# The second MLP's first product of tokens 1024 to 3071 in seven block products for eight, weight block sums through DRAM

## The chip, the cores and the metric

The kernel runs on one core of a Trainium2 chip. The metric is the device time of one execution in microseconds (us). A core has a matrix engine (TensorE, PE in the profile), three engines for elementwise work (VectorE or DVE, ScalarE or ACT, GpSimd or POOL), a queue engine that only starts transfers (SyncE, SP), an on-chip memory (SBUF, 128 partitions) and eight accumulation banks for PE (PSUM). Each engine executes its own instructions in a fixed order and waits on semaphores for the others.

## What is computed

The reference, cut to its core:

```python
def _moe_ref(x, w_gate, w_val, w_out):        # d_ff 1536
    gate = 1.0 / (1.0 + np.exp(-(x @ w_gate)))
    val = x @ w_val
    return (gate * val @ w_out).astype(np.float32)

def _moe2_ref(x, w_in, w_out):                # d_ff 2048
    h = x @ w_in
    g = h * (1.0 / (1.0 + np.exp(-1.702 * h)))
    return (g @ w_out).astype(np.float32)

def reference(**kwargs):
    ...
    attn_out = _attn_ref(**attn_kwargs)
    B, H, S, D = attn_out.shape
    x = np.ascontiguousarray(attn_out.transpose(0, 2, 1, 3)).reshape(B * S, H * D)
    x = _moe_ref(x=x, **moe_kwargs)
    return _moe2_ref(x=x, **moe2_kwargs)
```

`_attn_ref` is attention in chunks of 32 queries over a short context (4 batches, 8 heads, 768 positions of 64 values). It gives x with 3072 tokens of 512 values. The first MLP multiplies sigmoid(x w_gate) by x w_val and projects back to 512; the second computes h = x w_in with 2048 columns, h * sigmoid(1.702 h), and projects back to 512.

## The kernel before

**Precision.** PE multiplies rounded operands, so each float32 operand is cut into a high part and a low part, and each product is three matmuls: high by high, high by low, low by high. The inputs arrive as 64-bit numbers; `convert` loads 512 KB of a weight (`raw`) and turns it on ACT, DVE and POOL into a slot `w` that holds the highs and the lows of 128 rows or columns (lines 258 to 291: L258 load, L262 and L272 ACT, L267, L276 and L281 DVE, L286 the high on ACT, L291 the low on DVE or POOL).

**Tiling.** Tokens are handled in six blocks of 512. A matmul has 128x128 weights and 512 columns of tokens. For each slice f of 128 hidden columns, `first_product` makes 12 matmuls: 8 for the highs of the weight (L742), 4 for the lows (L749), over four parts of the depth of 512. In the second MLP there are 16 slices in each block. `gated` then takes the product from its bank: sigmoid on ACT (L766, `sig`), multiplication by the product on DVE (L769, into `sig`), the high `gh` on ACT (L772), the low `gl` (L776) on POOL in the second MLP's block 0, on DVE elsewhere. `gemm4` is the second product of a slice, 12 matmuls (L720), added up over the 16 slices in four banks. `sig`, `gh` and `gl` have two buffers each, and the first products of the second MLP alternate between two banks.

**Between the MLPs.** The first MLP's result goes from its banks by ACT (L937) to DRAM (`y_dram`, L941) and comes back a block at a time in `y_in`: four loads (L957), four highs on ACT (L960, `xh`), four lows on POOL (L963, `xl`). After the last block ACT (L1045) and DVE (L1043) empty the banks and SP stores the output (L1049).

**Order.** Every step is handed to the class `Schedule` as a task with an engine, a modelled duration and the data that it reads and writes. A planner then gives each engine a fixed order: among the ready tasks of an engine it takes the one with the earliest due time. A PE product's due time is the sum of the modelled durations of the products handed in before it (`clock[0]`), and other tasks inherit theirs from what needs them. The planner's durations decide the order alone; on the chip each engine goes through its order and waits where something isn't there. The weights of the second MLP are converted while the first MLP's products run; its slots come free as the first MLP's weights are used up.

The functions that the change touches and what calls them, with the profile's line numbers:

Of the kernel before, what the change touches and what calls it, by code (L numbers as in the profile page):

```python
# [1103 lines left out]
```

## Time and profile before

| what | value |
|---|---|
| device time, median of 3 runs | 1220.63 us (1219.94 to 1221.95) |
| span of the profiled execution, first to last instruction | 1217.7 us |
| PE, busy share of the span | 98% |
| DVE, busy share | 51% |
| ACT, busy share | 39% |
| POOL, busy share | 10% |
| mean granted clock of PE | 0.994 |

The page gives the profiled execution's span, and its device time is not listed apart from it; the median of the runs lies 2.9 us above the span. The busy shares are means over stages that differ: attention lies mostly in the first half, the conversion of the second MLP's weights ends at about 693 us, and the second MLP runs from there to the end. "Granted clock" is the clock that the chip gave PE, with 1.00 for 2.4 GHz. A duration in the timeline is that of one instruction, and instructions of one engine that follow each other overlap a little, so that their spacing is shorter than their duration.

### The profile page before, as it was taken

How to read it: one execution, taken by the hardware profiler on the slowest of the kernel's cores; microseconds unless marked ns; L12 is line 12 of the kernel's file. 1: busy time of each engine (PE TensorE's matmuls, PEld its weight loads, DVE VectorE, ACT ScalarE, POOL GpSimd, SP SyncE). 2: the span in 40 equal slices, each digit the busy share in tenths (PEclk: the TensorE clock that was granted, in tenths of full speed). 3: DMA queues.
4: the chain of work that ended last, by engine and by line, in shares of the span. 5: the costliest groups of instructions: out<-in, count | busy, mean ns of one | idle time of the engine just before them, and what ended most of it. 6: DMA issues, size and time to landing. Idle time of an engine off the chain costs nothing.

```text
span 1217.7 us, 18791 instructions
## 1 busy us (share of the span) xinstructions
PE 1195.5 (98%) x7448; PEld 997.8 (82%) x7448; DVE 622.6 (51%) x1282; ACT 481.0 (39%) x779; POOL 123.6 (10%) x112
## 2 busy tenths in 40 slices
PE   5899999999999999999999999999999999999998
PEld 4688899988888888888888888888888888888886
DVE  7898858883778448617888611222222222322322
ACT  5698734442334224413667632222222222322222
POOL 1221200000000000000211232110000100100000
PEclk9799999999999999999999999999999999999999
DMA  9566333333133113300555310100100100200001
GB/s 229 131 201 181 100 81 54 53 54 70 34 52 79 24 22 58 80 1 23 152 185 169 121 52 1 53 18 1 65 5 1 69 1 1 70 1 1 35 1 36
DMA packets 169673, 78.01 MB, mean 64 GB/s; under 512 B 136176, under 2 KB 156912, under 8 KB 169584
## 3 DMA queue, kind: packets, MB, share of 16 engines
q1 hardware_dynamic: 166128, 70.51, 22.6%
q10 hardware_dynamic: 3456, 6.29, 1.4%
q8 instruction: 58, 0.95, 0.3%
q14 instruction: 31, 0.25, 0.1%
HBM read 64.18 MB, written 12.58 MB: 63 GB/s over the span
## 4 chain that ended last, share of the span: by engine, by line
PE 96%; DVE 2%; DMA 1%; ACT 1%; issue 0%; SPq 0%; DVEq 0%
PE bank L742 35%; PE bank L720 21%; PE bank L749 18%; PE bank L917 16%; PE bank L656 2%; PE bank L506 2%; PE bank L596 1%; DMA raw<-in_moe_w_gate_dram 0%; DVE pw L574 0%; PE bank L397 0%; DMA qn<-in_q_dram 0%; PE bank L389 0%; DVE e L526 0%; DVE mx L523 0%; DVE sm L563 0%
## 5 line engine op out<-in xcount | busy, mean ns | idle before, releaser
L742 PE MATMUL bank<-xh,w 128*128 128x512 f32 (+1 forms) x1040 | 383.5, 374 | 2.8 <-ACT w L286 1.6
L742 PE MATMUL bank<-xl,w 128*128 128x512 f32 (+1 forms) x1040 | 382.3, 373 | 0.0
L769 DVE TENSOR_TENSOR sig<-bank,sig 128x512 f32<-128x512 f32 (+1 forms) x178 | 117.4, 660 | 410.4 <-ACT sig L766 328.9
L749 PE MATMUL bank<-xh,w 128*128 128x512 f32 (+1 forms) x1040 | 260.1, 374 | 0.0
L766 ACT ACTIVATE sig<-bank 128x512 f32<-128x512 f32 (+1 forms) x178 | 102.4, 575 | 386.7 <-PE bank L749 378.1
L720 PE MATMUL bank<-w,gh 128*128 128x512 f32 x768 | 236.5, 389 | 0.0
L742 PEld LDWEIGHTS bank<-xh,w 128*128 128x128 f32 x1040 | 195.7, 188 | 39.1 <-ACT w L286 2.3
L742 PEld LDWEIGHTS bank<-xl,w 128*128 128x128 f32 x1040 | 195.9, 188 | 34.3
L749 PEld LDWEIGHTS bank<-xh,w 128*128 128x128 f32 x1040 | 186.0, 188 | 35.0
L772 ACT ACTIVATE gh<-sig 128x512 fp32r<-128x512 f32 (+1 forms) x178 | 108.1, 607 | 187.0 <-DVE sig L769 170.2
L720 PEld LDWEIGHTS bank<-w,gh 128*128 128x128 f32 x768 | 144.1, 188 | 29.9
L917 PE MATMUL bank<-gh,w 128*128 128x512 f32 (+1 forms) x656 | 158.2, 365 | 0.0
L776 DVE TENSOR_TENSOR gl<-sig,gh 128x512 fp32r<-128x512 f32 (+1 forms) x162 | 110.2, 680 | 84.7 <-ACT gh L772 73.0
L720 PE MATMUL bank<-w,gl 128*128 128x512 f32 x384 | 149.4, 389 | 0.0
L917 PEld LDWEIGHTS bank<-gh,w 128*128 128x128 f32 x656 | 114.4, 189 | 19.8
L720 PEld LDWEIGHTS bank<-w,gl 128*128 128x128 f32 x384 | 72.1, 188 | 15.0
L631 DVE STREAM_TRANSPOSE pt<-raw 32x256 f32<-32x256 f32 x184 | 80.1, 435 | 2.8
L917 PE MATMUL bank<-gl,w 128*128 128x512 f32 (+1 forms) x328 | 80.4, 367 | 0.0
L917 PEld LDWEIGHTS bank<-gl,w 128*128 128x128 f32 x328 | 56.8, 189 | 9.9
L574 POOL TENSOR_TENSOR raw<-e,sm 96x448 f32<-96x448 f32 x23 | 23.2, 1007 | 405.6 <-DVE sm L566 405.6
L963 POOL TENSOR_TENSOR xl<-f,xh 128x512 fp32r<-128x512 f32 x24 | 31.0, 1301 | 276.6 <-ACT xh L960 276.6
L286 ACT ACTIVATE w<-f 128x512 fp32r<-128x512 f32 x68 | 42.7, 640 | 13.2 <-DVE f L281 9.1
(84 smaller groups left out, 822.1 us busy)
## 6 DMA issues: line engine op xcount, KB each, us to landing
raw<-in_moe_w_out_dram SPq DMA_DIRECT2D x24, 512.0 KB
raw<-in_moe_w_in_dram SPq DMA_DIRECT2D x16, 512.0 KB
y_dram<-f ACTq DMA_DIRECT2D x24, 256.0 KB
f<-y_dram SPq DMA_DIRECT2D x24, 256.0 KB
out_dram<-f SPq DMA_DIRECT2D x23, 256.0 KB
vn<-in_v_dram SPq DMA_DIRECT2D x24, 240.0 KB
f<-in_q_dram SPq DMA_DIRECT2D x276, 16.0 KB
raw<-in_moe_w_gate_dram SPq DMA_DIRECT2D x8, 512.0 KB
```

Of the source, the lines that this page charges most:

```text
L286: nc.scalar.activation(slots[slot][:, 0, :], ft, AF.Copy)
L506: nc.tensor.matmul(bk[c * CH : (c + 1) * CH, p * KW : (p + 1) * KW], T["qt"][r, p, c * CH : (c + 1) * CH], T["kt"][r, p, c, :], start=True ...
L631: nc.vector.transpose(T["pt"][r * CH : (r + 1) * CH, :, c * CH : (c + 1) * CH], T["pn"][c * CH : (c + 1) * CH, :, kb * CH : (kb + 1) * CH],)
L720: nc.tensor.matmul(ps_out, a, c, start=(first and i == 0 and j == 0), stop=(last and i == n - 1 and j == 2),)
L742: nc.tensor.matmul(bank[bk][:, :n], w[:, 0, ts[t]], x[xb][:, t, c0 : c0 + n], start=t == 0 and x is xhs, stop=False)
L749: nc.tensor.matmul(bank[bk][:, :n], w[:, 1, ts[t]], xhs[xb][:, t, c0 : c0 + n], start=False, stop=t == NK - 1)
L766: nc.scalar.activation(sig[:, :n], bank[src_sig][:, :n], AF.Sigmoid, scale=scale)
L769: nc.vector.tensor_tensor(out=sig[:, :n], in0=bank[src_val][:, :n], in1=sig[:, :n], op=ALU.mult)
L772: nc.scalar.activation(gh[:, :n], sig[:, :n], AF.Copy)
L776: eng.tensor_tensor(out=gl[:, :n], in0=sig[:, :n], in1=gh[:, :n].bitcast(F32), op=ALU.subtract)
L917: nc.tensor.matmul(bank[Y[m]][:, c0 : c0 + n], w[:, wi, m * P : (m + 1) * P], g[:, :n], start=f == 0 and j == 0 and c0 == 0, stop=f == F1 ...
L963: nc.gpsimd.tensor_tensor(out=xls[xb][:, m, :], in0=st[:, :BLK], in1=xhs[xb][:, m, :].bitcast(F32), op=ALU.subtract)
```

## The change

The first product of blocks 0 and 1 of the second MLP stays as it is. Blocks 2 to 5 are taken as two superblocks of two blocks. For two slices (a pair j, eight of them) and two blocks, the depth of 512 in two halves, the product is one of 2x2 blocks of weights with 2x2 blocks of tokens. Winograd's form of Strassen's scheme needs seven products (`m1` to `m7`, `part_product`, 6 matmuls each) of sums of the blocks for the eight of the direct way.

- `combine(j)` makes the sums of weight blocks of a pair, once: POOL adds highs and lows back to whole numbers (`cw_a`, `cw_b`), DVE makes four sums of 256 columns (`cw_s`) and, after ACT has cut the highs (`cw_h`), the lows (`cw_l`). SP writes three ready blocks and the four sums of each pair to DRAM (`wc_dram`).
- `fetch` brings the seven blocks of a pair back, 256 KB each, into a ring of 14 that lies in freed slots, once for each superblock.
- `x_prep` makes the sums of token blocks for a superblock: 8 loads, 8 subtractions on DVE, 14 highs on ACT, 14 lows on POOL and DVE.
- In the loop over pairs the products share banks, so that PE does part of the additions by accumulating. `snap` copies a bank to SBUF on ACT, `plus` adds another bank on DVE; `gate2` makes the sigmoid and the multiplication. The first block's two results go on to `halves` (`gh` and `gl`, as before), the second block's are kept as `gBs` until the pairs are through; then their halves and second products follow.

```diff
-    def gemm4(b, f, i):
+    def gemm4(f, i, banks, row, end=False, after=()):
...
+    NBP = 2
+    NSB = (NB2 - NBP) // 2
+    NPR = F2 // 2
+    NMP = 7
...
+    STEPS = {"m1": (MA11, XB11), "m5": (MS1, XT1), "m6": (MS2, XT2), "m2": (MA12, XB21),
+             "m3": (MS4, XB22), "m7": (MS3, XT3), "m4": (MA22, XT4)}
+    SEQ = ["m1", "m5", "m6", "m2", "m3", "m7", "m4"]
...
+    def combine(j):
+        s0, s1 = slot_in2[2 * j], slot_in2[2 * j + 1]
+
+        def whole(x, s):
+            def fn():
+                w = slots[s]
+                nc.gpsimd.tensor_tensor(out=cw[x], in0=w[:, 0, :].bitcast(F32), in1=w[:, 1, :].bitcast(F32), op=ALU.add)
+
+            add("pool", c_pool(512), fn, r=[("w", s, 0), ("w", s, 1)], w=["c" + x])
...
+        def sums():
+            wa, wb, s = cw["wa"], cw["wb"], cw["s"]
+            tt = nc.vector.tensor_tensor
+            tt(out=s[:, 0, :], in0=wb[:, :H2], in1=wb[:, H2:], op=ALU.add)
+            tt(out=s[:, 2, :], in0=wa[:, :H2], in1=wb[:, :H2], op=ALU.subtract)
+            tt(out=s[:, 1, :], in0=s[:, 0, :], in1=wa[:, :H2], op=ALU.subtract)
+            tt(out=s[:, 3, :], in0=wa[:, H2:], in1=s[:, 1, :], op=ALU.subtract)
+
+        def high():
+            nc.scalar.activation(cw["h"], cw["s"], AF.Copy)
...
+        for m, s, c in ((MA11, s0, 0), (MA12, s0, H2), (MA22, s1, H2)):
+            put(m, 1, None, lambda s=s, c=c: slots[s][:, :, c : c + H2].bitcast(F32), [("w", s, 0), ("w", s, 1)])
+        put(MS1, 4, 0, lambda: cw["h"].bitcast(F32), ["cwh"])
+        put(MS1, 4, 1, lambda: cw["l"].bitcast(F32), ["cwl"])
+
+    for j in range(NPR):
+        combine(j)
...
+    def part_product(g, m, bk, first):
+        h = (g * NMP + SEQ.index(m)) % NRH
+        x = STEPS[m][1]
+
+        def fn():
+            w = ringh[h]
+            for k in range(2):
+                for wl, xl in ((0, 0), (0, 1), (1, 0)):
+                    o = wl * H2 + k * P
+                    nc.tensor.matmul(
...
-    for b in range(NB2):
+    for b in range(NBP):
...
+            part_product(g, "m1", a, True)
+            snap("s1", a)
+            part_product(g, "m5", e, True)
+            snap("s5", e)
+            if fill:
+                gemm4(*fill.pop(0))
+            part_product(g, "m6", a, False)
+            snap("s2", a)
+            part_product(g, "m2", bb, True)
+            plus("s1", bb)
+            ia = gate2(lambda: work["s1"], "s1")
+            part_product(g, "m3", e, False)
+            plus("s2", e)
+            gate2(lambda: work["s2"], "s2", 2 * j)
+            part_product(g, "m7", a, False)
+            plus("s5", a)
+            gate2(lambda: work["s5"], "s5", 2 * j + 1)
+            if fill:
+                gemm4(*fill.pop(0))
+            part_product(g, "m4", a, False)
+            ic = gate2(lambda a=a: bank[a], ("bank", a))
+            if g + 2 < NSB * NPR:
+                fetch(g + 2)
...
+        for f in range(F2):
+            gemm4(*fill.pop(0))
+            i = halves(lambda f=f: gbs[f], ("gB", f))
+            fill.append((f, i, ob, row + BLK, end))
```

In the changed file `combine`'s whole sums are L1093, its quarter sums L1103 to L1106, its highs L1109 and lows L1113, its writes L1126 and L1128; `fetch` is L1234, `part_product` L1248, `snap` L1260, `plus` L1264, the multiplication of `gate2` L1292, the low of `halves` L1278.

**POOL in block 0 of the second MLP.** The slices' `gl` take two buffers in turn (`gl_86`, `gl_87`); the last row is that of slice 8. Before, from block 1's second-last `xl` on:

```order
L963 TENSOR_TENSOR xl_735<-f_79,xh_734 128x512
L776 TENSOR_TENSOR gl_86<-sig_82,gh_84 128x512
L963 TENSOR_TENSOR xl_735<-f_80,xh_734 128x512
L776 TENSOR_TENSOR gl_87<-sig_83,gh_85 128x512
L776 TENSOR_TENSOR gl_86<-sig_82,gh_84 128x512
L776 TENSOR_TENSOR gl_87<-sig_83,gh_85 128x512
L776 TENSOR_TENSOR gl_86<-sig_82,gh_84 128x512
```

The same stretch in the changed kernel, from slice 5's `gl` on:

```order
L776 TENSOR_TENSOR gl_87<-sig_83,gh_85 128x512
L1093 TENSOR_TENSOR cw_b<-w_642 128x512
L963 TENSOR_TENSOR xl_736<-f_80,xh_735 128x512
L1093 TENSOR_TENSOR cw_a<-w_644 128x512
L1093 TENSOR_TENSOR cw_b<-w_646 128x512
L776 TENSOR_TENSOR gl_86<-sig_82,gh_84 128x512
L1093 TENSOR_TENSOR cw_a<-w_648 128x512
L1093 TENSOR_TENSOR cw_b<-w_650 128x512
L776 TENSOR_TENSOR gl_87<-sig_83,gh_85 128x512
L1093 TENSOR_TENSOR cw_a<-w_652 128x512
L1093 TENSOR_TENSOR cw_b<-w_654 128x512
L776 TENSOR_TENSOR gl_86<-sig_82,gh_84 128x512
```

The last row is the `gl` of slice 8. Since the last conversion (L291) 28 instructions stand ahead of it: 16 whole sums, 8 `gl` and 4 `xl`; before, 12 stood ahead of it.

**DVE from the last conversions on.** Before, the multiplications of the second MLP's slices 0, 1, 2 follow the last conversions directly:

```order
L776 TENSOR_TENSOR gl_87<-sig_83,gh_85 128x512
L291 TENSOR_TENSOR w_653<-f_77,w_653 128x512
L281 SCALAR_TENSOR_TENSOR f_78<-f_78,raw_75 128x512
L769 TENSOR_TENSOR sig_82<-bank_66,sig_82 128x512
L291 TENSOR_TENSOR w_654<-f_78,w_654 128x512
L769 TENSOR_TENSOR sig_83<-bank_67,sig_83 128x512
L769 TENSOR_TENSOR sig_82<-bank_66,sig_82 128x512
```

In the changed kernel the sums and lows of the weights stand between them:

```order
L291 TENSOR_TENSOR w_655<-f_78,w_655 128x512
L1103 TENSOR_TENSOR cw_s<-cw_b 128x256
L1104 TENSOR_TENSOR cw_s<-cw_a,cw_b 128x256
L1105 TENSOR_TENSOR cw_s<-cw_s,cw_a 128x256
L1106 TENSOR_TENSOR cw_s<-cw_a,cw_s 128x256
L769 TENSOR_TENSOR sig_83<-bank_67,sig_83 128x512
L1113 TENSOR_TENSOR cw_l<-cw_s,cw_h 128x512 x2
L1103 TENSOR_TENSOR cw_s<-cw_b 128x256
L1104 TENSOR_TENSOR cw_s<-cw_a,cw_b 128x256
L1105 TENSOR_TENSOR cw_s<-cw_s,cw_a 128x256
L1106 TENSOR_TENSOR cw_s<-cw_a,cw_s 128x256
L769 TENSOR_TENSOR sig_82<-bank_66,sig_82 128x512
```

The multiplication of slice 1 now stands behind pair 0's sums, and that of slice 2 (last row) behind pair 1's.

**PE in the loop over pairs (changed kernel only).** `bank_67` is the bank of `m1`, `m6`, `m7`, `m4` here, `bank_73` that of `m5` and `m3`, `bank_66` that of `m2`. The rows run from the end of a second product (slice 8's, weight `w_641`) over `m6`, `m2`, `m3` and `m7` to the next:

```order
L720 MATMUL bank_71<-w_641,gl_86 128x512
L1248 MATMUL bank_67<-sb_x_6708,sb_r_7658 128x512 x3
L1248 MATMUL bank_67<-sb_x_6762,sb_r_7658 128x512 x3
L1248 MATMUL bank_66<-sb_x_6657,sb_r_7697 128x512 x3
L1248 MATMUL bank_66<-sb_x_6681,sb_r_7697 128x512 x3
L1248 MATMUL bank_73<-sb_x_7322,sb_r_7697 128x512 x3
L1248 MATMUL bank_73<-sb_x_7346,sb_r_7697 128x512 x3
L1248 MATMUL bank_67<-sb_x_7387,sb_r_7728 128x512 x3
L1248 MATMUL bank_67<-sb_x_7433,sb_r_7728 128x512 x3
L720 MATMUL bank_68<-w_643,gh_85 128x512 x2
```

After that second product `m4` writes into `bank_67`, which `plus` of `s5` reads once `m7` is through. Before, a slice there had 12 matmuls of L742 and L749 and then 12 of L720.

## Rows read from the trace of the kernel before

**Rows 1.** The page: span, busy time by engine, slices of PE and its clock.

```profile
span 1217.7 us, 18791 instructions
PE 1195.5 (98%) x7448; PEld 997.8 (82%) x7448; DVE 622.6 (51%) x1282; ACT 481.0 (39%) x779; POOL 123.6 (10%) x112
...
PE   5899999999999999999999999999999999999998
...
PEclk9799999999999999999999999999999999999999
```

**Rows 2.** The page: chain that ended last, shares by engine and line.

```profile
PE 96%; DVE 2%; DMA 1%; ACT 1%; issue 0%; SPq 0%; DVEq 0%
PE bank L742 35%; PE bank L720 21%; PE bank L749 18%; PE bank L917 16%; PE bank L656 2%; PE bank L506 2%; PE bank L596 1%; DMA raw<-in_moe_w_gate_dram 0%; DVE pw L574 0%; PE bank L397 0%; DMA qn<-in_q_dram 0%; PE bank L389 0%; DVE e L526 0%; DVE mx L523 0%; DVE sm L563 0%
```

**Rows 3.** Stretches: length, busy time (count) by engine, clock, DMA share, GB/s.

```profile
28.00:44.00 16.00, 11.28 (x96) 9.70 (x96) 14.39 (x33) 7.29 (x14) 3.15 (x3) 0.57 0.14 54
...
630.00:730.00 100.00, 100.00 (x443) 82.81 (x442) 54.67 (x88) 58.02 (x89) 23.62 (x18) 1.00 0.37 116
730.00:830.00 100.00, 100.00 (x443) 82.81 (x442) 20.54 (x29) 24.91 (x42) 16.75 (x13) 1.00 0.06 22
830.00:930.00 100.00, 100.00 (x443) 82.81 (x442) 28.25 (x40) 26.57 (x44) 5.13 (x4) 1.00 0.06 22
```

**Rows 4.** Timeline of PE at 701: start, duration, engine, line, operands, count.

```profile
701.82 0.62 PE L720 MATMUL bank<-w,gh 128*128 128x512 f32 x2
```

**Rows 5.** Chain that ended last, its longest pieces: start, duration, what.

```profile
785.40 2.72 PE bank L720 x12
...
1207.90 5.47 PE bank L720 x24
```

**Rows 6.** Timeline of POOL, from 599 to 707 us.

```profile
599.82 1.30 POOL L963 TENSOR_TENSOR xl<-f,xh 128x512 fp32r<-128x512 f32 x1 [2.01 <-ACT xh L960]
...
677.70 1.29 POOL L291 TENSOR_TENSOR w<-f,w 128x512 fp32r<-128x512 f32 x1 [6.83 <-ACT w L286]
686.85 1.30 POOL L291 TENSOR_TENSOR w<-f,w 128x512 fp32r<-128x512 f32 x1 [7.86 <-ACT w L286]
...
705.28 1.29 POOL L776 TENSOR_TENSOR gl<-sig,gh 128x512 fp32r<-128x512 f32 x1 [5.56 <-ACT gh L772]
706.53 1.29 POOL L963 TENSOR_TENSOR xl<-f,xh 128x512 fp32r<-128x512 f32 x1
```

**Rows 7.** Timeline of DVE, from 599 to 702 us.

```profile
599.86 1.81 DVE L291 TENSOR_TENSOR w<-f,w 128x512 fp32r<-128x512 f32 x1
...
628.73 0.43 DVE L267 TENSOR_SCALAR raw<-raw 128x512 int32<-128x512 int32 x1 [1.76 <-DMA raw<-in_moe_w_in_dram]
...
678.45 0.69 DVE L769 TENSOR_TENSOR sig<-bank,sig 128x512 f32<-128x512 f32 x1 [1.79 <-PE bank L749]
...
688.95 0.68 DVE L776 TENSOR_TENSOR gl<-sig,gh 128x512 fp32r<-128x512 f32 x1
689.55 0.68 DVE L291 TENSOR_TENSOR w<-f,w 128x512 fp32r<-128x512 f32 x1
...
701.81 0.69 DVE L769 TENSOR_TENSOR sig<-bank,sig 128x512 f32<-128x512 f32 x1 [4.75 <-ACT sig L766]
```

**Rows 8.** Groups by line and shape: count, busy us, mean ns, idle before.

```profile
L526 DVE TENSOR_TENSOR e<-bank,mx 96x256 f32<-96x256 f32 x64 | 23.8, 410 | 0.1
...
L772 ACT ACTIVATE gh<-sig 128x512 fp32r<-128x512 f32 x158 | 99.8, 632 | 166.0 <-DVE sig L769 160.7 <-PE bank L720 3.9 <-ACT f L937 1.4
L766 ACT ACTIVATE sig<-bank 128x512 f32<-128x512 f32 x158 | 94.7, 599 | 365.0 <-PE bank L749 364.7
L410 ACT ACTIVATE kt<-bank 128x384 f32<-128x384 f32 x9 | 4.5, 501 | 5.3 <-PE bank L397 5.2
L411 ACT ACTIVATE kt<-bank 128x96 f32<-128x96 f32 x9 | 2.2, 249 | 0.0
```

**Rows 9.** Timeline of SP's queue: a weight load is issued.

```profile
624.88 0.38 SPq L258 DMA_DIRECT2D raw<-in_moe_w_in_dram  x1
```

More of the change, by code (lines that the diff above doesn't have):

```diff
@@ L1028, in gemm4 @@
             fn,
-            [("w", s, 0), ("w", s, 1), ("gh", i), ("gl", i)] + after,
-            [("bank", O[b][tt]) for tt in range(TT)],
+            [("w", s, 0), ("w", s, 1), ("gh", i), ("gl", i), *after],
+            [("bank", k) for k in banks],
         )
@@ new lines, in fetch, with fn @@
+    def fetch(g):
+        for p, m in enumerate(SEQ):
+            h = (g * NMP + p) % NRH
+            src = g % NPR * NMP + STEPS[m][0]
+            def fn(h=h, src=src):
+                nc.sync.dma_start(out=ringh[h].bitcast(F32), in_=wc_dram[src])
+            kr = [("wc", g % NPR, STEPS[m][0], x) for x in range(2)]
+            add("sp", 0.45, fn, r=kr, w=[("ring", h)], nbytes=P * 512 * 4)
+    def part_product(g, m, bk, first):
+        h = (g * NMP + SEQ.index(m)) % NRH
+        x = STEPS[m][1]
+        def fn():
+            w = ringh[h]
+            for k in range(2):
+                for wl, xl in ((0, 0), (0, 1), (1, 0)):
+                    o = wl * H2 + k * P
+                    nc.tensor.matmul(
+                        bank[bk],
+                        w[:, o : o + P],
+                        xt[x, k][:, xl, :],
+                        start=first and k == 0 and wl == 0 and xl == 0,
+                        stop=k == 1 and wl == 1,
+                        skip_group_check=not first,
+                    )
+        product(c_mm(512, 6), fn, [("ring", h)] + xkey(x), [("bank", bk)])
@@ L1067 @@
                 gemm4(*pend)
-            if f == 0 and b + 1 < NB2:
+            if f == 0 and b + 1 < NBP:
                 y_in(b + 1, (xb + 1) % 2)
-            pend = (b, f, i)
-    gemm4(*pend)
+            pend = (f, i, O[b], b * BLK)
+    nsig[0] = ngh[0] = ng[0]
+    x0 = NB % 2
+    add("none", 0.0, open_x0, w=xkeys(x0) + xkey(XB11) + xkey(XT1))
+    add("none", 0.0, open_work, w=KCW + KYS + ["s1", "s2", "s5", ("gB", 0), ("gB", 1)])
+    homes = [(m, k) for m in (XB21, XT2, XB22, XT3, XT4) for k in range(2)]
@@ new lines @@
+    assert 2 * len(left[NRH // 2 :]) + 2 == 8
+    add("none", 0.0, open_x1b, w=xkeys(1 - x0) + [("gB", f) for f in range(8, 16)])
+    sets = [[6, 7, 0, 1], [2, 3, 4, 5]]
+    assert sorted(O[NBP - 1]) == sets[1]
+    fill = [pend]
+    fetch(0)
+    fetch(1)
+    for sb in range(NSB):
+        a0, e, bb, a1 = sets[sb % 2]
+        oa = sets[1 - sb % 2]
+        ob = [bb, e, a0, a1]
+        row = (NBP + 2 * sb) * BLK
+        ready = []
+        for j in range(NPR):
+            g = sb * NPR + j
+            a = (a0, a1)[j % 2]
+            part_product(g, "m1", a, True)
[21 more added lines that the diff above has]
+                fetch(g + 2)
+            fill += [(2 * j, ia, oa, row), (2 * j + 1, ic, oa, row)]
+        if sb + 1 < NSB:
+            x_prep(NBP + 2 * sb + 2)
+        end = sb == NSB - 1
+        for f in range(F2):
+            gemm4(*fill.pop(0))
+            i = halves(lambda f=f: gbs[f], ("gB", f))
+            fill.append((f, i, ob, row + BLK, end))
```

152 lines of the change are left out of this document (147 added, 5 removed).

## The prediction

> **What bounds the kernel now.** I read the page first: TensorE (PE) is busy for 98% of the span, no other engine for more than 51%, and the granted clock stands at its upper level in all slices but one [rows 1]. The chain that ended last is 96% PE, and its largest line, L742, is the first products [rows 2]. Then I read the busy time by stretches: in the second MLP each stretch of 100 us holds 100.00 us of PE, with VectorE (DVE), ScalarE (ACT) and GpSimd (POOL) at 5 to 58%; in the stretch 630 to 730, with five times the DMA traffic of the next (116 against 22 GB/s), PE runs just as full [rows 3]. So from about 630 us the time is matmuls times their spacing, and whatever is taken out there shortens the span, unless PE then begins to wait. The clock's mean fell to 0.57 (1.00 is the level of 2.4 GHz, 0.50 that of 1.2) only at 28 to 44 us, where PE was busy for 11.28 of 16 us [rows 3]; waits of a microsecond or two are not of that kind, and I charge no clock.
>
> The spacing: the first second-product of the second MLP starts at 701.82 [rows 4], the last group starts at 1207.90 and lasts 5.47, to 1213.37 [rows 5]. The second MLP has 6 blocks x 16 slices x 24 = 2304 matmuls, of which 48 run before 701.82 (the first products of four slices). (1213.37 - 701.82) / 2256 = 0.2267 us each, and 12 then take 2.72, as the chain shows [rows 5].
>
> **The change, part by part.** *Removed:* for each pair of slices of two blocks, 8 half-depth products of 6 matmuls become 7: 48 to 42. With 8 pairs and 2 superblocks this is 16 x 6 = 96 matmuls, 96 x 0.2267 = **21.8 us**. Nothing else on PE changes in number: the new ones are 128x128 by 512 columns too, with one weight load each, as before.
>
> *Added on POOL, DVE and ACT in block 0 of the second MLP:* `combine` builds four sums of weight blocks for each of 8 pairs. This is 16 whole sums on POOL, 32 quarter sums (256 columns) and 16 lows (512) on DVE, 8 highs of 1024 columns on ACT. All stand in the queues where block 0's gating stands, and block 0 cuts its `gl` on POOL. In the order the POOL op that cuts `gl` of slice 8 now has 28 others ahead of it that may start only after the last weight conversion (16 sums, 8 earlier `gl`, 4 `xl`); before it had 12 of them. The price hangs on one thing: whether DVE and POOL can work at once. The rows say no, for DVE instructions that read two operands from SBUF: POOL's L963 starts at 599.82 and lasts 1.30 [rows 6], and DVE's L291, begun at 599.86, takes 1.81 [rows 7], where the same line alone takes 0.68 (689.55) [rows 7]; the surplus of 1.13 is about what was left of the POOL instruction. A DVE multiplication that reads one operand from PSUM took its normal 0.69 at 678.45 [rows 7], inside POOL's L291 at 677.70 [rows 6]. The sums and lows are of the held kind. So I add POOL and DVE up, as one queue.
>
> This queue starts when POOL's last conversion ends, 686.85 + 1.30 = 688.15 [rows 6], and ends with `gl` of slice 8. It holds 29 POOL instructions, the quarter sums of seven pairs (28) and the lows of six (12), since the whole sums of pair 7 wait for the quarter sums of pair 6, and these for the lows of pair 5. By durations: 29 x 1.29 [rows 6] + 28 x 0.41 (L526, 256 columns [rows 8]) + 12 x 0.68 [rows 7] = 37.4 + 11.5 + 8.2 = 57.1, so 745.2. By spacings of instructions back to back, which overlap a little: POOL 1.25 (705.28 to 706.53 [rows 6]); DVE 0.60 (688.95 to 689.55 [rows 7]), thus 0.08 less than a duration, and 0.33 for 256 columns: 36.3 + 9.2 + 7.2 = 52.7, so 740.9. PE needs that `gl` in the second product of slice 8: in the new order the fifth slice's first product stands where the first second-product stood, so at 701.82 if nothing waits, and 170 matmuls later the matmul reads `gl`: 701.82 + 170 x 0.2267 = 740.4. The stall is thus between **0.5** and **4.8 us**. To that comes ACT's high of 1024 columns, which stands between sums and lows: from 96 columns in 0.249 and 384 in 0.501 [rows 8], 0.875 ns a column, some 1.06 us. Where POOL has its next whole sums and gating to do meanwhile it is covered, else not; I take it as covered in six of the first seven pairs, which leaves 1.1; uncovered in all seven it is 7.4. I take durations, not spacings, since at each change between the two engines there is a handover and no overlap: 4.8 + 1.1 = **5.9 us**, bounds 0.5 and 4.8 + 7.4 = 12.2. What is late after that is only PE; the `gl` of slices 9 to 15 follow with one POOL instruction per 24 matmuls (5.4 us).
>
> The Trainium skill (Advanced Engine Details and Errata, VectorE Performance Modes) says that GpSimd and VectorE share a second SBUF port and hold each other up, but only for VectorE instructions in a two-port mode, and its table gives tensor_tensor none. By that rule the sums would run beside POOL. The row of L291, a TENSOR_TENSOR, at 1.81 speaks against the narrow reading; the section GPSIMD Details of the same page has the wider one (two SBUF inputs), which agrees. By the narrow rule the time would be that of the first rival below.
>
> A smaller wait lies ahead of it: the multiplication of slice 2 stands behind the quarter sums of pair 1 on DVE. It ran at 701.81 before [rows 7] and the fifth slice's first product reuses its bank; 0 to 1 us, inside the same stall and not added to it.
>
> *Added DMA:* 8 x (3 x 256 + 2 x 512) KB written, 14.7 MB, and 16 x 7 x 256 KB read, 29.4 MB. In the loop 7 x 256 KB come per pair of 66 matmuls (42 first, 24 second), 15.0 us: 123 GB/s, like the 116 GB/s beside which PE ran full [rows 3]. The ring holds two pairs, so a fetch has about one pair, 15 us, where a 512 KB load took from its issue at 624.88 [rows 9] to its use at 628.73 [rows 7], 3.9 us. Cost nothing, covered by the other half of the ring. The writes of ready weights stand among the raw loads in SP's queue, each behind a conversion that those loads wait for anyway: 0 to 1 us on conversions that are used much later. Nothing.
>
> *Added in the loop:* per pair DVE has 9 instructions of 0.69 (6.2 us) and ACT 9 of about 0.6 (5.4 us), in 15.0 us of PE. The tightest place is `m4`, which writes into the bank that `plus s5` still reads. `m2`, `m3`, `m7` take 1.36 us each. From the end of `m2`: `plus s1` to 0.69, sigmoid (0.60 [rows 8]) to 1.3, `plus s2` from 1.36 to 2.05, the multiplication to 2.74, `plus s5` to 3.43. PE has the second product of 12 (2.72) after `m7`, and comes to `m4` at 2.72 + 2.72 = 5.44. Slack 2.0 us: hidden. `m6` waits for the snapshot of `m1` and has `m5` and a second product between, 4.1 us against 0.6: hidden. `x_prep` (8 loads, 8 subtractions, 14 highs, 14 lows) runs in block 1, where DVE had 28.25 us of work in 100 (830 to 930 [rows 3]), for its first call, and under sixteen second products (43.5 us) for the second: hidden. The final run of second products needs one high (0.63 [rows 8]) and one low (0.68 [rows 7]) per 2.72 us: hidden. Without this cover each place would cost its own microsecond or two per pair.
>
> **Sum.** The profiled execution has a span of 1217.7; the median is 1220.63, so 2.9 us lie around the span, and I keep them. 1220.6 - 21.8 + 5.9 = **1204.7** (a span of 1201.8).
>
> **The rivals.** *A, the sums are hidden:* POOL and DVE do not hold each other, or the alternation overlaps more than I say, and 0.5 to 0.9 us stay: 1220.6 - 21.8 + 0.5 to 0.9 = 1199.3 to 1199.7. For it: the lower bound by spacings. Against: the 1.81. *B, the stall is larger:* ACT's highs lie bare in each pair, and with semaphores between three engines it exceeds 12.2: 1211 to 1218. For it: the chain sums, high, lows, sums has three engines and single buffers. Against: POOL has other work to do meanwhile. *C, slower:* in each of the 16 pairs `m4` waits for `plus s5`, because DVE takes its work in a fixed order and the multiplication ahead waits for ACT, which itself stands behind a snapshot or a high of the pair before. With the slack of 2.0 used up and exceeded by 1.5 us: 16 x 1.5 = 24 us, so 1204.7 + 24 = 1228.7; it turns the change to no gain from (21.8 - 5.9) / 16 = 1.0 us per pair. Against: the engines in that loop are idle for half of the time. *D, it doesn't take 96 away:* excluded, the new order has 6328 PE matmuls against 6424.
>
> **Chances.** Forecast case 0.60 (1200 to 1211), A 0.22, B 0.11, C 0.07, of which 0.03 end within 0.2% of before. This kernel's measurement can tell 0.2%, 2.4 us, from no change. Faster 0.93, same 0.03, slower 0.04. The range takes in A and the forecast case with its upper bound, 1220.6 - 21.8 + 12.2 = 1211.0, and a little of B: 1198.5 to 1212.5.
>
> **What would show it.** PE idle for 3 to 10 us in all between 700 and 750, ended by POOL's `gl` (L776) or a DVE multiplication (L769), and none to speak of after 760; L1093 on POOL and L1103 to L1113 on DVE with means above 1.29, 0.41 and 0.68; L1248 672 times, L742 1568 and L749 784 times; the clock 1.00 throughout. I am wrong if PE waits in the loop of pairs (for `sb_r`, a late fetch, or for L1264 in front of `m4`), or if L1093 and L1113 have their plain durations while PE still waits.

## The result and the profile after

The changed kernel takes 1208.45 us (median of 4 runs, 1207.04 to 1209.51) against 1221.29 of the kernel before: 12.8 us less, a ratio of 0.9897 with a 95% interval of 0.9883 to 0.9911. The forecast was 1204.7 with a range of 1198.5 to 1212.5. The profiled execution has a span of 1207.7.

The page of the changed kernel: span, busy time, shares of the chain that ended last (to compare with [rows 1, 2]).

```profile
span 1207.7 us, 19184 instructions
PE 1180.2 (98%) x7352; PEld 982.2 (81%) x7352; DVE 712.2 (59%) x1406; ACT 522.2 (43%) x847; POOL 153.3 (13%) x128
...
PE 90%; DVE 5%; ACT 2%; issue 1%; DMA 1%; POOL 0%; DVEq 0%; SPq 0%; ACTq 0%; POOLq 0%
```

PE has 96 instructions fewer (7352 for 7448), and is still busy for 98%. What is new is the second engine in the chain: DVE with 5% where it had 2%, and ACT with 2% where it had 1%. So PE now waits for them somewhere. The busy time by stretches says where (columns as in [rows 3]: length, busy time of PE, PE's weight loads, DVE, ACT and POOL, clock, DMA share, GB/s):

```profile
700.00:720.00 20.00, 19.22 (x85) 15.58 (x84) 16.13 (x22) 9.21 (x15) 13.98 (x10) 1.00 0.74 250
720.00:740.00 20.00, 19.57 (x87) 15.84 (x86) 13.88 (x18) 7.98 (x13) 16.38 (x13) 1.00 0.44 145
740.00:747.00 7.00, 5.07 (x23) 3.82 (x21) 6.39 (x8) 2.18 (x3) 5.45 (x4) 1.00 0.45 151
747.00:752.00 5.00, 4.70 (x14) 3.75 (x15) 3.52 (x7) 1.58 (x2) 1.80 (x2) 0.66 0.56 189
752.00:760.00 8.00, 8.00 (x37) 6.60 (x36) 0.69 (x1) 1.48 (x3) 1.12 (x2) 1.00 0.66 210
...
940.00:950.00 10.00, 10.00 (x46) 8.29 (x45) 3.18 (x5) 2.94 (x5) 0.00 (x0) 1.00 0.37 109
...
980.00:990.00 10.00, 9.24 (x41) 7.32 (x41) 7.93 (x9) 5.59 (x11) 6.42 (x4) 1.00 0.50 135
990.00:1000.00 10.00, 9.04 (x39) 6.82 (x38) 9.81 (x12) 6.47 (x12) 4.84 (x3) 1.00 0.29 104
```

There are two places: block 0 of the second MLP (700 to 752), with a fall of the granted clock to 0.66 in one stretch, and the second `x_prep` (980 to 1000). At both POOL has work; in the loop between them (940 to 950) it has none, and PE is full. PE's timeline names what it waited for (in brackets: idle time ahead of the instruction, and what ended it):

```profile
705.39 0.50 PE L742 MATMUL bank<-xh,w 128*128 128x512 f32 x1 [0.78 <-DVE sig L769]
738.85 0.50 PE L742 MATMUL bank<-xh,w 128*128 128x512 f32 x1 [0.43 <-DVE sig L769]
747.30 0.50 PE L720 MATMUL bank<-w,gl 128*128 128x512 f32 x1 [2.23 <-POOL gl L776]
748.39 1.06 PE L720 MATMUL bank<-w,gh 128*128 128x512 f32 x2
749.67 1.06 PE L720 MATMUL bank<-w,gh 128*128 128x512 f32 x2
...
989.35 0.50 PE L720 MATMUL bank<-w,gl 128*128 128x512 f32 x1 [0.76 <-DVE gl L1278]
993.64 0.50 PE L720 MATMUL bank<-w,gl 128*128 128x512 f32 x1 [0.84 <-DVE gl L1278]
1059.28 3.04 PE L1248 MATMUL bank<-sb_x,sb_r 128*128 128x512 f32 x12 [0.52 <-ACT sb_s L1260]
```

Two matmuls in a row took 1.06 at 748.39 and 749.67, where [rows 4] has 0.62: these ran at the lower clock. Taking the spacing of neighbouring matmuls less 0.2267 for each, I get the time lost at each place: 1.05 at 705, 0.70 at 739, 2.51 at 747 (each wait and the slower first matmul behind it), 1.60 from 748.1 to 751.8 for the clock, together **5.9** in block 0; 0.93 + 0.11 + 0.29 + 1.13 + 0.10 = **2.6** at 988 to 994; 0.68 + 0.11 = **0.8** at 1059. That is 9.2 us (the expectations below, written with the wait at 1059 taken as 0.7, say 9.1).

**A measure for all runs.** The second MLP starts at a time that differs from run to run (700.0 to 703.2 in the profiles below) although the order up to there is nearly the same, so I don't compare spans. I take the time from the last weight-low group ahead of the second products (8 matmuls of L749, at 700.01 before, 1.81 ahead of the row of [rows 4]) to the start of the last matmul, and take off the number of matmuls between times their spacing before, (1212.97 - 700.01) / 2263 = 0.2267. What is left is lost.

| kernel | L749 group at | last matmul at | matmuls between | lost us | median us (before beside it) |
|---|---|---|---|---|---|
| before | 700.01 | 1212.97 | 2263 | 0 (by definition) | 1221.29 |
| changed | 702.64 | 1203.43 | 2167 | 9.6 | 1208.45 (1221.29) |
| changed, once more | 701.57 | 1202.36 | 2167 | 9.6 | 1207.73 (1222.17) |
| e1: whole sums on DVE | 703.22 | 1202.52 | 2167 | 8.1 | 1206.87 (1220.66) |
| e3: and block 0's gl on DVE | 702.73 | 1198.18 | 2167 | 4.3 | 1204.06 (1220.66) |
| e4: x_prep's lows on DVE | 702.29 | 1200.71 | 2167 | 7.2 | 1205.55 (1220.66) |
| e5: all three | 700.87 | 1194.05 | 2167 | 2.0 | 1200.00 (1222.17) |
| e6: one pair's sums only | 701.18 | 1196.74 | 2167 | 4.4 | 1203.35 (1220.66) |
| e9: whole sums of 16 columns | 701.18 | 1196.72 | 2167 | 4.3 | 1202.23 (1221.02) |
| e7: one superblock | 701.74 | 1208.78 | 2215 | 5.0 | 1215.63 (1222.17) |
| e10: one superblock, once more | 702.14 | 1209.15 | 2215 | 4.9 | 1215.19, one run (1221.02) |
| e8: the kernel before with four waits made | 701.95 | 1234.64 | 2263 | 19.7 | 1240.58, one run (1222.17) |

For the changed kernel 21.8 - 9.6 = 12.2 us should be gained, and the medians give 12.8. Of the changed kernel's 9.6 the places above hold 9.2; the other 0.4 I can't put at a place. The difference of the two spans, 10.0, is smaller since the changed kernel's profile started its second MLP 2.6 us later. That comes from far ahead of the change: 2.4 of the 2.6 us are there at PE's 1000th matmul, in attention (136.35 against 133.95 us), and e8, with the order of the kernel before up to there, reaches it at 136.00.

### The profile page after: what moved, and what is told of

Same layout as the page of the kernel before. It is cut to its first block, busy times and chain, and to the rows that moved or that the text cites. A ratio compares the mean times of both kernels' runs of the same rounds, so it can differ in the third digit from the quotient of the medians.

```text
span 1207.7 us, 19184 instructions
## 1 busy us (share of the span) xinstructions
PE 1180.2 (98%) x7352; PEld 982.2 (81%) x7352; DVE 712.2 (59%) x1406; ACT 522.2 (43%) x847; POOL 153.3 (13%) x128
## 4 chain that ended last, share of the span: by engine, by line
PE 90%; DVE 5%; ACT 2%; issue 1%; DMA 1%; POOL 0%; DVEq 0%; SPq 0%; ACTq 0%; POOLq 0%
PE bank L742 25%; PE bank L720 19%; PE bank L917 16%; PE bank L749 12%; PE bank L1248 12%; PE bank L656 2%; PE bank L506 2%; DVE cw_l L1113 1%; DVE cw_s L1103 1%; PE bank L596 1%; ACT cw_h L1109 0%; DVE pw L574 0%; PE bank L397 0%; DVE cw_s L1104 0%; PE bank L389 0%
## 5 line engine op out<-in xcount | busy, mean ns | idle before, releaser
L742 PE MATMUL bank<-xh,w 128*128 128x512 f32 (+1 forms) x784 | 284.7, 370 | 3.5 <-ACT w L286 1.6
L742 PE MATMUL bank<-xl,w 128*128 128x512 f32 (+1 forms) x784 | 282.9, 368 | 0.0
L720 PE MATMUL bank<-w,gh 128*128 128x512 f32 x768 | 237.7, 391 | 0.1
L749 PE MATMUL bank<-xh,w 128*128 128x512 f32 (+1 forms) x784 | 191.7, 370 | 0.0
L742 PEld LDWEIGHTS bank<-xh,w 128*128 128x128 f32 x784 | 148.0, 189 | 31.6 <-DVE sig L769 2.8
L720 PEld LDWEIGHTS bank<-w,gh 128*128 128x128 f32 x768 | 144.5, 188 | 30.7 <-ACT gh L1275 0.6
L742 PEld LDWEIGHTS bank<-xl,w 128*128 128x128 f32 x784 | 147.9, 189 | 24.2
L769 DVE TENSOR_TENSOR sig<-bank,sig 128x512 f32<-128x512 f32 (+1 forms) x114 | 73.1, 641 | 154.9 <-PE bank L749 80.2
L749 PEld LDWEIGHTS bank<-xh,w 128*128 128x128 f32 x784 | 138.0, 188 | 24.9
L720 PE MATMUL bank<-w,gl 128*128 128x512 f32 x384 | 150.3, 392 | 3.8 <-POOL gl L776 2.2
L917 PEld LDWEIGHTS bank<-gh,w 128*128 128x128 f32 x656 | 114.4, 189 | 19.7
L772 ACT ACTIVATE gh<-sig 128x512 fp32r<-128x512 f32 (+1 forms) x114 | 67.4, 592 | 138.2 <-DVE sig L769 121.9
L766 ACT ACTIVATE sig<-bank 128x512 f32<-128x512 f32 (+1 forms) x114 | 63.9, 560 | 139.5 <-PE bank L749 130.7
L1248 PE MATMUL bank<-sb_x,sb_r 128*128 128x512 f32 x480 | 115.8, 389 | 0.5 <-ACT sb_s L1260 0.5
L1248 PEld LDWEIGHTS bank<-sb_x,sb_r 128*128 128x128 f32 x480 | 90.0, 188 | 19.6 <-ACT sb_s L1260 0.9
L720 PEld LDWEIGHTS bank<-w,gl 128*128 128x128 f32 x384 | 72.3, 188 | 20.1 <-POOL gl L776 2.7
L776 DVE TENSOR_TENSOR gl<-sig,gh 128x512 fp32r<-128x512 f32 (+1 forms) x98 | 64.9, 662 | 37.2 <-ACT gh L772 26.6
L1264 DVE TENSOR_TENSOR sb_s<-bank,sb_s 128x512 f32<-128x512 f32 x48 | 33.1, 691 | 62.4 <-PE bank L1248 54.3
```

The source lines that it names most:

```text
L720: nc.tensor.matmul(ps_out, a, c, start=(first and i == 0 and j == 0), stop=(last and i == n - 1 and j == 2),)
L742: nc.tensor.matmul(bank[bk][:, :n], w[:, 0, ts[t]], x[xb][:, t, c0 : c0 + n], start=t == 0 and x is xhs, stop=False)
L749: nc.tensor.matmul(bank[bk][:, :n], w[:, 1, ts[t]], xhs[xb][:, t, c0 : c0 + n], start=False, stop=t == NK - 1)
L766: nc.scalar.activation(sig[:, :n], bank[src_sig][:, :n], AF.Sigmoid, scale=scale)
L769: nc.vector.tensor_tensor(out=sig[:, :n], in0=bank[src_val][:, :n], in1=sig[:, :n], op=ALU.mult)
L772: nc.scalar.activation(gh[:, :n], sig[:, :n], AF.Copy)
```

## The experiments

**The theory:** DVE instructions with two operands from SBUF and POOL's instructions hold each other up; in block 0 the sums of weights on both engines and the gating make one queue, and at the second `x_prep` POOL's lows hold DVE. **The rivals:** in block 0 the chain of quarter sums on DVE, high on ACT, lows on DVE sets the pace, whatever POOL does; at `x_prep` loads come late, or DVE has too much to do.

**e1, the whole sums on DVE** instead of POOL (for each POOL instruction of 1.29 one of 0.69 on DVE).

```diff
-                nc.gpsimd.tensor_tensor(out=cw[x], in0=w[:, 0, :].bitcast(F32), in1=w[:, 1, :].bitcast(F32), op=ALU.add)
+                nc.vector.tensor_tensor(out=cw[x], in0=w[:, 0, :].bitcast(F32), in1=w[:, 1, :].bitcast(F32), op=ALU.add)
...
-            add("pool", c_pool(512), fn, r=[("w", s, 0), ("w", s, 1)], w=["c" + x])
+            add("dve", c_dve(512), fn, r=[("w", s, 0), ("w", s, 1)], w=["c" + x])
```

> The 16 whole sums of weights (L1093) go from POOL to DVE, everything else stays. Theory (POOL and DVE share a port, and block 0's gl of slice 8 stands behind both engines' work): POOL holds DVE only for its 13 gl and xl in block 0, the queue up to gl of slice 8 is 16 x 0.60 + 28 x 0.33 + 12 x 0.60 + 13 x 1.25 = 42.3 us instead of 52.7 to 57.1, and PE's wait in block 0 (5.9 us with the slow matmuls behind it) falls to 0 to 1.5: 1202.6 to 1204.1 us. Rival (the chain sums on DVE, high on ACT, lows on DVE, next sums sets the pace, not the port): DVE's part of the chain grows by 1.2 us per pair, so the time stays or rises, 1208 to 1213 us.

1206.87 us, 8.1 us lost: neither expectation. The wait for `gl` of slice 8 (the last row here) is down from 2.23 to 0.50, and the clock no longer falls behind it, but PE now waits longer at two other places. PE's waits in this kernel:

```profile
706.81 0.50 PE L742 MATMUL bank<-xh,w 128*128 128x512 f32 x1 [1.62 <-DVE sig L769]
729.49 0.50 PE L720 MATMUL bank<-w,gl 128*128 128x512 f32 x1 [0.16 <-POOL gl L776]
734.96 0.50 PE L742 MATMUL bank<-xh,w 128*128 128x512 f32 x1 [1.07 <-DVE sig L769]
748.02 0.50 PE L720 MATMUL bank<-w,gl 128*128 128x512 f32 x1 [0.50 <-POOL gl L776]
```

The multiplication of slice 2 now stands behind the whole sums of pair 2 as well, in DVE's order, and one quarter sum (L1106) was still held by a POOL `gl`. DVE's timeline ahead of the wait at 706.81, and the POOL instruction beside it:

```profile
703.01 1.39 DVE L1106 TENSOR_TENSOR cw_s<-cw_a,cw_s 128x256 f32<-128x256 f32 x1
704.86 0.69 DVE L1093 TENSOR_TENSOR cw_a<-w 128x512 f32<-128x512 f32 x1 [0.46 <-DVE cw_s L1106]
705.47 0.68 DVE L1093 TENSOR_TENSOR cw_b<-w 128x512 f32<-128x512 f32 x1
706.07 0.68 DVE L769 TENSOR_TENSOR sig<-bank,sig 128x512 f32<-128x512 f32 x1
```

```profile
702.82 1.30 POOL L776 TENSOR_TENSOR gl<-sig,gh 128x512 fp32r<-128x512 f32 x1 [5.07 <-ACT gh L772]
```

So the move took most of the wait for the late `gl` away and made others out of it, since the planner's order put more in front of a multiplication that PE needs. It doesn't decide between theory and rival.

**e3, block 0's gl on DVE too** (`gated(..., False)` for all blocks of the second MLP, beside e1's edit).

> As the run with the whole sums on DVE, and block 0's gl (L776) on DVE too; POOL keeps the 4 xl. Theory: no POOL work of length beside the sums, DVE instructions at their plain durations (0.69 for 512 columns, 0.41 for 256), PE waits less than 1 us in block 0: 1202.6 to 1203.5 us. Rival (the three-engine chain): DVE has all work in one row, 1208 to 1214 us.

1204.06 us, 4.3 us lost: 0.6 above the theory's range, 3.9 below the rival's. From 700 to 760 PE's idle time falls to half a microsecond, although DVE has 18 and 19 us of work in the first two stretches of 20 us:

```profile
700.00:720.00 20.00, 19.49 (x86) 15.85 (x85) 17.97 (x30) 10.05 (x17) 3.98 (x3) 1.00 0.76 252
720.00:740.00 20.00, 20.00 (x90) 16.56 (x89) 19.12 (x36) 8.92 (x13) 1.47 (x1) 1.00 0.58 196
740.00:760.00 20.00, 20.00 (x90) 16.55 (x89) 9.86 (x16) 5.50 (x10) 1.30 (x1) 1.00 0.39 132
```

This is against the rival: the chain of sums, high and lows has all its instructions, DVE has 16 whole sums and block 0's `gl` on top, and PE no longer waits for it. By the groups of 680 to 760, the first quarter sum (L1103) took 1096 ns on the mean in the changed kernel, where POOL worked beside it, and 417 ns here:

```profile
L1113 DVE TENSOR_TENSOR cw_l<-cw_s,cw_h 128x512 fp32r<-128x512 f32 x16 | 17.5, 1122 | 6.3 <-ACT cw_h L1109 4.3 <-DMA wc_dram<-cw_l 2.0
L1103 DVE TENSOR_TENSOR cw_s<-cw_b 128x256 f32<-128x256 f32 x8 | 8.8, 1096 | 4.3 <-POOL cw_b L1093 4.3
```

```profile
L1113 DVE TENSOR_TENSOR cw_l<-cw_s,cw_h 128x512 fp32r<-128x512 f32 x16 | 11.8, 755 | 2.7 <-DMA wc_dram<-cw_l 1.9 <-ACT cw_h L1109 0.8
...
L1103 DVE TENSOR_TENSOR cw_s<-cw_b 128x256 f32<-128x256 f32 x8 | 3.3, 417 | 0.0
```

(The first fence is the changed kernel, the second e3; columns: count, busy us, mean ns, idle time before and its releasers.)

**e9, the whole sums of 16 columns instead of 512**, all instructions and their order on every engine as in the changed kernel, but for two fills of zeros on POOL (0.53 us each) ahead of the first pair's sums. It parts theory and rival without a new order.

```diff
-                w = slots[s]
-                nc.gpsimd.tensor_tensor(out=cw[x], in0=w[:, 0, :].bitcast(F32), in1=w[:, 1, :].bitcast(F32), op=ALU.add)
+                w = slots[s]; j or nc.gpsimd.memset(cw[x], 0.0)
+                nc.gpsimd.tensor_tensor(out=cw[x][:, :16], in0=w[:, 0, :16].bitcast(F32), in1=w[:, 1, :16].bitcast(F32), op=ALU.add)
```

> POOL's whole sums (L1093) add only 16 of the 512 columns of a weight slice, all other instructions and their order stay as in the changed kernel (POOL fills the two tiles with zeros once, ahead of the first sum); the output of tokens 1024 to 3071 is not the reference's. Theory (in block 0 PE waits for POOL's and DVE's instructions together, since they hold each other): the queue up to gl of slice 8 loses 16 x about 1.2 us, POOL's gl comes in time, DVE's quarter sums and lows go at nearly their plain durations; the 5.9 us lost in block 0 fall to 0 to 1, 1202.3 to 1203.5 us on a chip where the kernel before takes 1221. Rival (the chain of quarter sums on DVE, high on ACT, lows on DVE sets the pace of block 0): this chain keeps all its instructions, 4 to 6 us stay lost, 1206.5 to 1208.5 us.

1202.23 us, 4.3 lost; in block 0 only 0.8 us, at 704. The chain that the rival names is all there; what went is 19.0 us of POOL's time (16 whole sums, 23.8 us together before, 4.8 now). This is against the rival. But one part of the expectation is not borne out: of the DVE instructions that were held, only the first quarter sum (L1103) came down to its plain duration. By the groups of 680 to 760 in e9:

```profile
L1113 DVE TENSOR_TENSOR cw_l<-cw_s,cw_h 128x512 fp32r<-128x512 f32 x16 | 14.9, 965 | 7.1 <-DMA wc_dram<-cw_l 4.6 <-ACT cw_h L1109 1.7 <-ACT f L937 0.8
L1104 DVE TENSOR_TENSOR cw_s<-cw_a,cw_b 128x256 f32<-128x256 f32 x8 | 6.6, 830 | 0.0
L1103 DVE TENSOR_TENSOR cw_s<-cw_b 128x256 f32<-128x256 f32 x8 | 3.3, 418 | 3.4 <-POOL cw_b L1093 3.4
```

L1104 took 827 ns in the changed kernel, L1106 425 there and 698 here; POOL's `gl` and `xl` still run beside them. So e9 shows that without POOL's time in the whole sums the `gl` comes in time, and e3 and the durations show that the two engines hold each other. POOL's time alone would not make it late: its 29 instructions of 1.29 are 37.4 us, and from 690.4, where its queue begins, to 745.1, where PE came for that `gl`, there are 54.7. It is POOL's and DVE's time together: theory.

**e6, one pair's sums only.**

```diff
-    for j in range(NPR):
+    for j in range(1):
         combine(j)
...
-            src = g % NPR * NMP + STEPS[m][0]
+            src = STEPS[m][0]
```

> The sums of weight blocks are made for the first pair of slices only and its blocks are fetched for every pair: 14 whole sums, 28 quarter sums, 14 lows, 7 highs and their writes are left out, and the output of tokens 1024 to 3071 is not the reference's. Theory: block 0's loss (5.9 us) is the price of these sums, and what is left is x_prep's 2.6 and a snapshot's 0.7: 1202.0 to 1203.0 us. Rival (the loss in block 0 comes from the changed order of PE or from the transfers beside it): 1206 to 1209 us.

1203.35 us, 4.4 lost, with 0.8 in block 0: 0.4 above the theory's range, far from the rival's. The order of PE's products and the fetches cost nothing there (the writes went with the sums here; in e9 they are all there, and 0.8 us is lost too). The sums cost 9.6 - 4.4 = 5.2 us.

**e4, x_prep's lows on DVE** (`cut(..., False)` in all seven places; four had `True`).

> The 8 lows per superblock that x_prep cuts on POOL (L1192) go to DVE, everything else stays. Theory (at 981 to 994 us PE waits for gl because POOL's lows hold DVE's subtractions and multiplications): the 2.6 us lost there vanish, DVE's instructions there take 0.69 instead of 1.2 to 1.8: 1205.5 to 1206.5 us. Rival 1 (x_prep's inputs come late, its loads stand behind four fetches in SP's queue): the loss stays, 1208 to 1209 us. Rival 2 (DVE simply has too many instructions there): the loss grows by some of 8 x 0.6 us, 1209 to 1212 us.

1205.55 us, 7.2 lost, 2.4 less than the changed kernel; of the 2.6 us at 988 to 994 some 0.3 stay. Both rivals fall: the loads are in SP's queue as before, and DVE has 8 instructions more and is done sooner. The changed kernel's timeline shows what held it. DVE:

```profile
983.50 0.68 DVE L1264 TENSOR_TENSOR sb_s<-bank,sb_s 128x512 f32<-128x512 f32 x1
984.10 1.19 DVE L1292 TENSOR_TENSOR sig<-sb_s,sig 128x512 f32<-128x512 f32 x1
985.21 0.68 DVE L1264 TENSOR_TENSOR sb_s<-bank,sb_s 128x512 f32<-128x512 f32 x1
985.81 1.18 DVE L1292 TENSOR_TENSOR xl_sb<-sb_s,sig 128x512 f32<-128x512 f32 x1
986.92 1.78 DVE L1209 TENSOR_TENSOR sb_y<-sb_y,sb_y 128x512 f32<-128x512 f32 x1
988.62 0.68 DVE L1278 TENSOR_TENSOR gl<-sig,gh 128x512 fp32r<-128x512 f32 x1
```

POOL beside it:

```profile
982.98 3.46 POOL L1192 TENSOR_TENSOR sb_x<-sb_y,sb_x 128x512 fp32r<-128x512 f32 x2
986.41 1.74 POOL L1192 TENSOR_TENSOR sb_x<-f,sb_x 128x512 fp32r<-128x512 f32 x1
```

`plus` (L1264) reads a bank of PSUM and takes 0.68 beside POOL; the multiplication and the subtraction with two SBUF operands take 1.18 to 1.78, and POOL's lows 1.74 instead of 1.29. The `gl` that PE waits for at 989.35 stands behind them. In e4 the same subtractions, by the groups of 970 to 1003:

```profile
L1209 DVE TENSOR_TENSOR sb_y<-sb_y,sb_y 128x512 f32<-128x512 f32 x4 | 2.7, 687 | 0.0
```

**e7, one superblock** (`NBP = 4`, and `sets = [[2, 3, 0, 1], [4, 5, 6, 7]]` for the banks), and **e10**, the same once more.

> Blocks 0 to 3 direct and only one superblock of two blocks: 48 matmuls fewer than before instead of 96 (10.9 us), the same sums of weights in block 0 in the same order on POOL, x_prep once instead of twice. Theory (the loss in block 0 belongs to the sums of weights, that at 981 to 994 us to the second x_prep, and both don't depend on the number of matmuls saved): 5.9 us lost in block 0, nothing at 980 to 1000, 0 to 0.7 elsewhere: 1220.7 - 10.9 + 5.9 to 6.6 = 1215.7 to 1216.4 us. Rival (the losses come per pair in the loop): half of 9.1, thus 1220.7 - 10.9 + 4.6 = 1214.4 us.

> The kernel with one superblock once more, word for word. In its first profile PE waited 2.23 us for gl of slice 8 and the granted clock stayed at 1.00 behind it, where the changed kernel's clock fell after the same wait in each of its profiles. Theory 1 (chance decides at a wait of this length): the clock may fall here, with 1.5 to 1.8 us lost behind it. Theory 2 (something in this kernel holds the clock up): it stays at 1.00 again.

1215.63 us for e7, and 1215.19 for e10's single run; 5.0 and 4.9 us lost, nearly all in block 0 (4.7), none at 980 to 1000. The 48 matmuls give 10.9 us. The median doesn't decide between theory and rival: beside a kernel before of 1222.17 they come to 1222.17 - 10.9 + 5.0 = 1216.3 and 1222.17 - 10.9 + 4.6 = 1215.9. The places do: with half the pairs gone, the loss in block 0 stayed, but for the clock, and that of the second `x_prep` and the one at 1059 are gone. The losses don't come per pair in the loop. Here PE waited 2.23 and 2.21 us at the same place as in the changed kernel, and the clock stayed at 1.00 behind the wait both times (e7, 747 to 752):

```profile
747.00:752.00 5.00, 4.80 (x22) 3.64 (x20) 2.62 (x5) 1.58 (x2) 1.82 (x1) 1.00 0.58 194
```

**e8, what a wait costs behind itself.** In the kernel before, the low of slice 8 is made 5, 7, 9 and 13 times over in blocks 1, 2, 3 and 4.

```diff
+        times = WAITS.get(ng[0], 1)
...
-            eng.tensor_tensor(out=gl[:, :n], in0=sig[:, :n], in1=gh[:, :n].bitcast(F32), op=ALU.subtract)
+            for _ in range(times):
+                eng.tensor_tensor(out=gl[:, :n], in0=sig[:, :n], in1=gh[:, :n].bitcast(F32), op=ALU.subtract)
```

> The kernel before, with the low of slice 8 (L776) made 5, 7, 9 and 13 times over on DVE in blocks 1, 2, 3 and 4 of the second MLP, so that PE waits there once in each, for four different times with 0.60 us for each repeat, less the slack. It measures what a wait of PE costs beyond itself. Theory (the half-rate matmuls at 748.4 to 751.7 us in the changed kernel follow from the wait of 2.2 us ahead of them): after a wait longer than 2.2 us the granted clock falls and some 1.7 us are lost on top, after one of 1.6 or less it does not. Rival (the clock there fell for another reason, as the transfers or the other engines' work): the clock stays 1.00 after every wait here.

1240.58 us in a single run, 19.7 lost. PE waited 0.78, 2.24, 3.69 and 6.60 us. The stretches behind these waits:

```profile
830.00:836.00 6.00, 6.00 (x28) 4.95 (x27) 1.38 (x2) 1.55 (x3) 0.00 (x0) 1.00 0.00 0
...
919.00:925.00 6.00, 6.00 (x19) 4.77 (x20) 0.22 (x1) 0.60 (x1) 0.00 (x0) 0.72 0.00 0
...
1012.00:1017.00 5.00, 5.00 (x16) 3.98 (x15) 0.00 (x0) 0.18 (x1) 0.00 (x0) 0.66 0.00 0
...
1107.00:1113.00 6.00, 5.81 (x17) 4.65 (x18) 0.13 (x1) 0.28 (x1) 0.00 (x0) 0.63 0.00 0
```

After 0.78 the clock stayed, after the three others it fell to the lower level for some 3 to 4 us, and each fall cost 1.6 to 2.0 us in matmuls of nearly double spacing (0.43 for 0.2267). The transfers stand still there (0 GB/s), and POOL too: no work of theirs brought the fall, it followed the wait. At 2.2 us it was not certain: it fell in the changed kernel (twice), in e4 and here, not in e7 and e10. What decides between them no run shows.

**e5, all three moves**: whole sums, block 0's `gl` and `x_prep`'s lows on DVE; of POOL's work in the second MLP the lows of `y` are left. With it the changed kernel once more, on the same chip.

> All three moves at once: whole sums (L1093), block 0's gl (L776) and x_prep's lows (L1192) on DVE; POOL keeps only the loads' lows of y (L963). Theory: the two losses are apart and both gone, 96 x 0.2267 = 21.8 us less than before and 0.1 to 0.4 lost in block 0, about 0.3 at the second x_prep, 0.7 at the snapshot after it: 1220.7 - 21.8 + 1.1 to 1.4 = 1200.0 to 1200.5 us, faster than the changed kernel by 7 to 8 us. Rival (DVE becomes the engine that PE waits for once all is on it): the losses come back at other places, 1203 to 1208 us.

> The changed kernel once more, word for word, beside the run with all three moves on one chip: 1207 to 1209.5 us. It is here for the difference between the two.

1200.00 us (1199.41 to 1202.10), a ratio to the kernel before of 0.9823 with an interval of 0.9808 to 0.9837. The changed kernel beside it took 1207.73 (1206.91 to 1209.43), a ratio to the kernel before of 0.9883 (0.9867 to 0.9900): 7.7 us more, like the difference of the losses, 9.6 - 2.0 = 7.6. Of the 2.0 lost, 0.8 are at 703, 0.3 at 984 and 0.8 at 1050. This version beats both. That the median falls on the forecast of 1200.0 is in part luck: the forecast had 1.1 to 1.4 lost and a kernel before of 1220.7, and with 2.0 and 1222.17 the sum is 1202.4; where the missing 2.4 us are, ahead of the second MLP or elsewhere, these runs don't settle.

## Why the prediction was right, and where it was not

- **96 matmuls, 21.8 us: right.** The last run of second products in the changed kernel has 216 matmuls, whose first and last start lie 48.79 us apart, 0.2269 each. The loop over pairs keeps PE full: 10.00 of 10.00 us at 940 to 950, beside 109 GB/s of transfers.
- **Block 0, 5.9 us: the mechanism right, the sum right by luck.** The step "POOL and DVE as one queue" is what e3, e9 and the durations show. The queue of 57.1 us by durations and 1.1 for ACT ran from 690.42 (POOL's last conversion) to 747.25 (end of slice 8's `gl`), 56.8 us. The stall itself was smaller than forecast, 4.3 us, as the queue was 1.4 shorter and began 0.4 earlier against PE. Its length came out by parts that differ from the forecast's: a cycle of three POOL instructions, four quarter sums and two lows took 6.24 us at 736 to 743 (POOL's rows below), which is the sum by spacings (3 x 1.25 + 4 x 0.33 + 2 x 0.60 = 6.3) and not that by durations (6.9); the rest are mainly times in which neither engine worked on the queue (3.2 us). The wait of the multiplication of slice 2, "0 to 1 us, inside the same stall", was 0.78 idle; in e6 and e9, where the stall is gone, 0.57 idle of it remain and cost 0.8 us of their own.

```profile
736.35 1.29 POOL L1093 TENSOR_TENSOR cw_a<-w 128x512 f32<-128x512 f32 x1 [1.55 <-DVE cw_s L1106]
742.59 1.30 POOL L1093 TENSOR_TENSOR cw_a<-w 128x512 f32<-128x512 f32 x1 [1.55 <-DVE cw_s L1106]
```

- **"Waits of a microsecond or two are not of that kind, and I charge no clock": wrong.** The clock fell behind the wait of 2.23 us and cost 1.6 us; e8 shows that such a fall follows a wait without any transfers. That the term for block 0 still came to 5.9 is these two errors set off against each other: 4.3 + 1.6 measured, 5.9 + 0 forecast.
- **"`x_prep` ... under sixteen second products for the second: hidden": wrong, 2.6 us.** This is the step that cost most. I found that POOL and DVE hold each other, and applied it to `combine` alone; `x_prep` puts 8 lows on POOL beside DVE's subtractions, and in the second call PE needs DVE's `gl` every 2.7 us. In the first call, in block 1, no time was lost. e4 takes it away.
- **The snapshots hidden: wrong once, 0.8 us.** I priced `m6` behind the snapshot of `m1` only. At 1059, in the second pair of the second superblock, it is `m3` that waits: it adds to the bank of `m5`, whose snapshot (ACT, L1260, 1058.63) may write its buffer only when the multiplication of the pair before (DVE, L1292, 1057.91 to 1058.60) has read it. In the other pairs it is hidden. This is the manner of rival C, a DVE multiplication late in a fixed order, at another product and once instead of sixteen times. It is read from the rows; no run takes this wait away by itself.

```profile
1057.91 0.69 DVE L1292 TENSOR_TENSOR sb_g<-sb_s,sig 128x512 f32<-128x512 f32 x1 [0.70 <-ACT sig L1289]
```

```profile
1058.63 0.60 ACT L1260 ACTIVATE sb_s<-bank 128x512 f32<-128x512 f32 x1 [0.27 <-DVE sb_g L1292]
```

- **The rest right:** the fetches (PE never waited for `sb_r`), `m4` behind `plus` of `s5`, the final run of second products, the conversions. Of the signs named ahead, PE's idle time at 700 to 750 (3.4 us, forecast 3 to 10) and what ended it came out, and so did the means of L1093 (1353 and 1628 ns), L1103 (1096), L1104 (827) and L1113 (1122); L1105 and L1106 stayed at about their plain duration (414 and 425). "None to speak of after 760" and "the clock 1.00 throughout" did not come out.

In sum the forecast lacked 2.6 + 0.8 us, and 0.7 because the kernel before takes 1221.29 rather than 1220.63 over more runs: 1204.7 + 4.1 = 1208.8, where 1208.45 were measured. The rivals: A (the sums hidden) falls by the 1096 ns of L1103, B (over 12.2 us in block 0) by the 5.9, C (`m4` waits in each pair) by a loop in which PE waits for no `plus`. By the wider rule of the Trainium skill (Advanced Engine Details and Errata, GPSIMD Details) two SBUF inputs are enough for a conflict with GpSimd; the rows of L1209 (1.78) and L1264 (0.68, one operand from PSUM) agree with it.
